# Routing search of the later experts in six passes of 3, 3, 3, 3, 2, 2 bits instead of eight of 2, with a place left out after a pass

## The chip, the cores and the metric

The kernel runs on one core of a Trainium2 chip. Its engines work side by side, each on its own queue in order: TensorE (PE in the rows, its weight loads PEld), VectorE (DVE), ScalarE (ACT), GpSimd (POOL), and SyncE (SP), which issues most transfers. The metric is device time in microseconds (us). The median of three runs before the change is 1104.6 us (1103.45 to 1105.63).

## The reference, cut to what matters

Three stages: windowed attention, a capacity-limited mixture of eight experts, a dense two-layer network. The change is in the routing of the mixture.

```python
logits = x @ w_gate                      # 3072 tokens, 8 experts
order = np.argsort(-logits.flatten())
for idx in order:                        # greedy: best pair first
    tok, e = idx // E, idx % E
    if assigned[tok] >= 0 or counts[e] >= cap:   # cap = 384
        continue
    assigned[tok] = e
    counts[e] += 1
...
for e in range(E):                       # own two layers, no overlap
    h = np.maximum(x[assigned == e] @ w1[e], 0.0)
    out[assigned == e] = h @ w2[e]
# then: h = x @ w_in; g = max(h, 0) + alpha * min(h, 0); g @ w_out
```

## The kernel before

Attention comes first and leaves the rows x in DRAM and the logits on the chip. Then `Experts.run` takes the experts one after the other, each with its 384 tokens in tiles of 3 x 128.

The greedy loop is replaced by phases, one for each expert (0 to 7). A phase finds the value of the 384th best pair of the expert that fills up next, marks that expert's tokens, turns them into a list, and closes the expert and the tokens in the logits. The value is a 32-bit key. `Router.phase` finds its upper 16 bits by one search and its lower 16 by a second; the last phase has no search, and phase 0 has one of its own (`first_search`), which the change leaves alone. So phases 1 to 6 make 12 searches.

A search (`Router.search`) makes eight passes, each of two bits. A pass compares all keys of a partition with three thresholds (`compare`, line 770: 8 experts x 3 thresholds x 24 tokens, 576 elements into `r_cmp`), adds them up along the tokens (`reduce`, line 778, into `r_red`), and adds up over the partitions by one small matmul on TensorE (`totals`, line 786, into `r_ps`). Then VectorE reads the totals (line 553, `r_mx`), counts the thresholds that are reached (line 556) and makes the next thresholds `r_thr` (line 564) and base (line 571) out of steps prepared beside the totals (`r_pre`, line 543). The last pass of a second search has four thresholds on float keys. A second search begins with `narrow` and `fill`, seven more small VectorE instructions.

The search is a generator, and its pieces are put between the matmuls. A yield follows the reduction and another follows the totals. An expert has 24 steps: 8 of its own first and second layer ("first-layer steps", matmuls on lines 923 and 950), and 16 of the dense network ("second-layer steps", lines 963 and 988). Step n issues the up-projection of step n+1 (12 matmuls) and then the down-projection of step n. A place for `next(gen)` stands at the start of a step, ahead of the up-projection, and one in the down-projection, ahead of its last third (`between`); two steps of an expert have none. That makes 44 places for an expert. All engines run in order, so TensorE stands still at the totals until the reduction is done, and VectorE takes up the evictions of a step's up-projection (lines 970 and 971 into `m_t`, or line 927 into `m_hh`) only behind the pieces issued before them. From `m_t` ScalarE makes the upper part of `m_g` (line 972) and GpSimd the lower part (line 973); the down-projection of the next step reads both. GpSimd also splits the experts' weights (line 891) and, for expert 0, the output weights (line 909). Late in an expert's second-layer steps the rows of the next expert are transposed (line 857) and evicted (lines 872 and 873).

The list of a phase takes six yields behind its searches: among them 24 small matmuls (line 704) on marks from VectorE (lines 686 to 697).

Of the kernel before, what the change touches and what calls it, by code (L numbers as in the profile page):

```python
# [9 lines left out]
FT = mybir.dt.float32  # L10
FR = mybir.dt.float32r
BF = mybir.dt.bfloat16
I32 = mybir.dt.int32
U32 = mybir.dt.uint32
U16 = mybir.dt.uint16
AF = mybir.ActivationFunctionType
OP = mybir.AluOpType
# [344 lines left out]
class Router:  # L362

    DIGITS = 3
    PASSES = 8
    BLOCK = 32
    CHUNK = 8
    CLOSED = 1.0e38
# [3 lines left out]
    def __init__(self, ctx, tc, logits, cap, n_experts, ident):  # L372
        nc = tc.nc
        self.nc, self.tc, self.L, self.cap, self.E = nc, tc, logits, cap, n_experts
        self.TT = logits.shape[1]
        E, TT, D = n_experts, self.TT, self.DIGITS
        assert cap == 3 * 128 and 2 * TT <= 128
        self.consts = consts = ctx.enter_context(tc.tile_pool(name="r_consts", bufs=1))
        self.m = consts.tile([128, TT], FT, name="r_m")
        self.flip = consts.tile([128, TT], I32, name="r_flip")  # L380
        self.key = consts.tile([128, TT], I32, name="r_key")
        halves = self.key.bitcast(U16).rearrange("p (t h) -> p t h", h=2)
        self.lo, self.hi = halves[:, :, 0], halves[:, :, 1]
        self.eq = consts.tile([128, E, TT], BF, name="r_eq")
        self.mk = consts.tile([128, E, TT], U16, name="r_mk")
        passes = self.HIGH + self.LOW
        self.cmp = consts.tile([128, max(E * (D + 1), max(d for d, _ in passes)) * TT], BF, name="r_cmp")
        both, at = consts.tile([128, sum(d for d, _ in passes)], U16, name="r_grid"), 0
        self.grids = []
        for d, _ in passes:  # L390
            self.grids.append(both[:, at:at + d])
            at += d
# [71 lines left out]
    def setup(self):  # L464
        nc, consts, E, TT, D = self.nc, self.consts, self.E, self.TT, self.DIGITS
        B = self.BLOCK
        NB = self.cap // B

        def iota(shape, dtype, name, pattern, base=0, slope=0):
            t = consts.tile(shape, dtype, name=name)  # L470
            nc.gpsimd.iota(t, pattern=pattern, base=base, channel_multiplier=slope,
                           allow_small_or_imprecise_dtypes=True)
            return t

        self.ones = consts.tile([128, 128], BF, name="r_ones")
        nc.vector.memset(self.ones, 1.0)
        self.before = consts.tile([128, 128], BF, name="r_before")
        nc.vector.memset(self.before, 1.0)
        nc.gpsimd.affine_select(self.before, self.before, pattern=[[1, 128]], compare_op=OP.is_gt, fill=0.0,
                                base=0, channel_multiplier=-1)  # L480
        self.slots = iota([128, B, TT], U16, "r_slots", [[1, B], [0, TT]])
        self.blocks = iota([128, NB, TT], U16, "r_blocks", [[1, NB], [0, TT]])
        yield
        self.tp = consts.tile([128, 2, TT], BF, name="r_tp")
        nc.gpsimd.iota(self.tp[:, 0], pattern=[[128, TT]], base=0, channel_multiplier=0,
                       allow_small_or_imprecise_dtypes=True)
        nc.gpsimd.iota(self.tp[:, 1], pattern=[[0, TT]], base=0, channel_multiplier=1,
                       allow_small_or_imprecise_dtypes=True)
        order = iota([128, E], FT, "r_order", [[-1, E]], base=E)
        self.flag = consts.tile([128, E, 5], FT, name="r_flag")  # L490
        nc.vector.tensor_scalar(self.flag[:, :, 4], order, 0.5 / E, None, op0=OP.mult)
        digits = iota([128, D, TT], FT, "r_digits", [[1, D], [0, TT]], base=1)
        self.last = iota([128, D + 1], FT, "r_last", [[1, D + 1]], base=1)
        yield
        for (d, size), g in zip(self.HIGH + self.LOW, self.grids):
            nc.gpsimd.iota(g, pattern=[[size, d]], base=size, channel_multiplier=0,
                           allow_small_or_imprecise_dtypes=True)
        yield
        ng = 128 // B
        rows = 2 * NB  # L500
        self.mask = consts.tile([rows, ng], BF, name="r_mask")
        t = iota([rows, ng], I32, "r_rows", [[-1, ng]], base=ng, slope=1)
        nc.vector.tensor_scalar(t, t, ng - 1, None, op0=OP.bitwise_and)
        nc.vector.tensor_scalar(self.mask, t, 0.0, None, op0=OP.is_equal)
        half = consts.tile([rows, 2, NB // ng], BF, name="r_half")
        t = iota([rows, 2, NB // ng], I32, "r_cols", [[-NB, 2], [-ng, NB // ng]], base=rows, slope=1)
        nc.vector.tensor_scalar(t, t, ng.bit_length() - 1, None, op0=OP.logical_shift_right)
        nc.vector.tensor_scalar(half, t, float(rows // ng), None, op0=OP.is_equal)
        self.unit = consts.tile([rows, NB // ng], BF, name="r_unit")
        nc.vector.tensor_tensor(self.unit, half[:, 0], half[:, 1], op=OP.add)  # L510
        yield
        self.steps = []
        for i in range(self.PASSES):
            step = consts.tile([128, D, TT], U16, name=f"r_step{i}")
            nc.vector.tensor_scalar(step, digits, self.size(i), None, op0=OP.mult)
            self.steps.append(step)
            if i % 3 == 2:
                yield
        yield
        self.ahead = consts.tile([128, 2 * TT], FT, name="r_ahead")  # L520
        nc.vector.memset(self.ahead, 0.0)
        self.units = consts.tile([128, 2 * TT], FT, name="r_units")
        nc.vector.memset(self.units, 1.0)

    def size(self, i):
        return float(4 ** (self.PASSES - 1 - i))

    def search(self, mk, result):
        nc, TT, D, w = self.nc, self.TT, self.DIGITS, self.work
        last = "top" in result  # L530
        thr, base, n = self.steps[0], None, self.PASSES
        for i in range(n):
            self.compare(result["full"] if last and i == n - 1 else mk, thr, 0, TT, TT)
            k = thr.shape[1]
            red = self.reduce(k)
            if last and i == n - 2:
                pre = w.tile([128, D + 1], FT, name="r_pre4")
                nc.vector.tensor_scalar(pre, self.last, base, None, op0=OP.add)
            elif i == 0:
                pre = self.steps[1]  # L540
            elif i < n - 1:
                pre = w.tile([128, D, TT], U16, name="r_pre")
                nc.vector.tensor_scalar(pre, self.steps[i + 1], base, None, op0=OP.add)
            if i == 0 and last:
                self.fill(result)
            yield
            cnt = self.totals(red, k)
            yield
            if last and i == n - 1:
                result["counts"], result["base"] = cnt, base  # L550
                return
            mx = w.tile([128, D], FT, name="r_mx")
            nc.vector.tensor_reduce(mx, cnt.rearrange("p e d -> p d e"), axis=AX.X, op=OP.max)
            ge = w.tile([128, D], FT, name="r_ge")
            dig = w.tile([128, 1], FT, name="r_dig")
            nc.vector.tensor_scalar(ge, mx, self.cap - 0.5, 0.0, op0=OP.is_ge, op1=OP.add, accum_out=dig)
            if i == n - 1:
# [2 lines left out]
                result["top"] = top  # L560
                return
            four = last and i == n - 2
            thr = w.tile([128, D + 1], FT, name="r_thr4") if four else w.tile([128, D, TT], U16, name="r_thr")
            nc.vector.scalar_tensor_tensor(thr, dig.to_broadcast([128, D + 1]) if four else  # L564
                                           dig[:, :, None].to_broadcast([128, D, TT]), self.size(i), pre,
                                           op0=OP.mult, op1=OP.add)
            nxt = w.tile([128, 1], FT, name="r_base")
            if base is None:
# [3 lines left out]
            base = nxt  # L572
# [200 lines left out]
    def reduce(self, d):  # L773
        nc, E = self.nc, self.E
        cmp = self.cmp[:, :E * d * self.TT].rearrange("p (e d t) -> p e d t", e=E, d=d)
        red = self.work.tile([128, E * 4], BF, name="r_red")[:, :E * d].rearrange("p (e d) -> p e d", d=d)
        with nc.allow_low_precision("counts up to 48 are exact in bfloat16"):
            nc.vector.tensor_reduce(red, cmp, axis=AX.X, op=OP.add)  # L778
        return red
# [19 lines left out]
class Experts:  # L799
# [206 lines left out]
    def run(self, router, n_experts):  # L1006
        nf1, nf2 = self.F1 // 128, self.F2 // 128
        routes = []
# [27 lines left out]
        def prepare(e, i):  # L1036
# [6 lines left out]
            else:  # L1043
                self.split_w2(e, 1)

        self.up1(0, 0)
        next(gen)
        self.split_w1(0, 2)
# [2 lines left out]
        for n, (e, s, f) in enumerate(steps):  # L1051
# [2 lines left out]
                self.load_w2(e, f + 3)  # L1054
            full = s == 1 and f == nf1 - 1 or s == 2 and f == 0
            if not full:
                next(gen, None)
            if s == 2 and chosen == e and len(routes) > e + 1 and "expert" in routes[e + 1]:
                chosen = e + 1
                self.choose(e + 1, routes[e + 1])  # L1060
# [21 lines left out]
                    self.split_w1(nx[0], nx[2] + 2)  # L1082
            for i in now:
                prepare(e + 1, i)
            (self.down1 if s == 1 else self.down2)(e, f, lambda: full or next(gen, None))
            if last:
                self.up2(e, 0)
            if s == 1 and f + 2 < nf1:
# [92 lines left out]
```

## Time and profile before

| | |
|---|---|
| median of three runs | 1104.6 us |
| the profiled execution | 1105.07 us |
| its span, first to last instruction | 1103.4 us |
| TensorE busy in the span | 1059.9 us (96%) |
| VectorE busy in the span | 761.8 us (69%) |
| GpSimd busy in the span | 516.1 us (47%) |

The rows are of one profiled execution. Times in rows count from the first instruction of the span. Busy time of TensorE holds its pipeline, and it is not the same as full use. Behind a duration stands, in brackets, idle time of the engine ahead of the instruction and what ended it. PEclk is the granted share of TensorE's clock, 1.00 being 2.4 GHz. A row of a stretch gives its bounds and length, then the busy us and the count of instructions of PE, PEld, DVE, ACT and POOL, then PEclk, the share of the transfer engines and GB/s. A row of a group ends with busy us, mean ns of one, and idle time ahead of it.

### The profile page before, as it was taken

Reading aid. Unit: us, or ns where it says so; the run is one execution under the profiler, and the core shown is the slowest. Engines: PE = TensorE matmul, PEld = TensorE weight load, DVE = VectorE, ACT = ScalarE, POOL = GpSimd, SP = SyncE. Lnnn points to the kernel's source line nnn. Section 1 sums busy time; section 2 is a strip of 40 time slices with the busy share of each in tenths; the row PEclk is TensorE's granted clock in tenths of the full one; section 3 lists DMA queues with packets and bytes.
Section 4 is the critical chain, followed back from the end, with each engine's and each line's share of the span. In section 5 each row is a group of like instructions: output and inputs, shape, how many; then the busy total and the mean of one; then the engine's idle time right before and its main releaser. Section 6 shows DMA issues by size and latency. Waiting matters only on the chain.

```text
span 1103.4 us, 19396 instructions
## 1 busy us (share of the span) xinstructions
PE 1059.9 (96%) x6658; PEld 939.1 (85%) x6659; DVE 761.8 (69%) x2228; ACT 401.4 (36%) x1001; POOL 516.1 (47%) x620
## 2 busy tenths in 40 slices
PE   8999999689999999999999999999999999999997
PEld 6877777559888988898889888988898999999995
DVE  7999999669879877887988798688752322231321
ACT  7999988223213321331133113312331232123211
POOL 4777776036457623542354326333533364246222
PEclk9999999769999999999999999999999999999998
DMA  9889985142244426334425333533354335334131
GB/s 221 221 234 229 230 239 134 30 120 66 110 172 143 163 77 200 105 134 142 155 96 182 125 115 115 162 131 125 99 162 143 134 98 194 130 115 162 64 127 67
DMA packets 151218, 156.54 MB, mean 142 GB/s; under 512 B 83536, under 2 KB 116304, under 8 KB 151120
## 3 DMA queue, kind: packets, MB, share of 16 engines
q1 hardware_dynamic: 147280, 142.72, 42.9%
q0 software_dynamic: 3840, 12.59, 3.4%
q8 instruction: 53, 0.87, 0.3%
q14 instruction: 45, 0.37, 0.1%
HBM read 134.31 MB, written 20.97 MB: 141 GB/s over the span
## 4 chain that ended last, share of the span: by engine, by line
PE 72%; DVE 14%; ACT 3%; issue 2%; DMA 1%; POOL 1%; SPq 0%; DVEq 0%; ACTq 0%; POOLq 0%
PE m_h L963 24%; PE m_acc L988 24%; PE m_acc L950 9%; PE m_h L923 9%; DVE a_sx L217 2%; DVE r_thr L564 2%; ACT a_p L220 2%; DVE r_red L778 1%; DVE r_cmp L770 1%; PE r_ps L704 1%; PE a_pt L231 1%; PE a_xp L247 1%; PE m_h L857 1%; PE a_s L211 1%; DVE f_t L78 1%
## 5 line engine op out<-in xcount | busy, mean ns | idle before, releaser
L973 POOL TENSOR_TENSOR m_g<-m_t,m_g 128x384 fp32r<-128x384 f32 (+1 forms) x144 | 139.8, 971 | 372.5 <-ACT m_g L972 370.5
L988 PE MATMUL m_acc<-m_so,m_g 128*128 128x512 f32 x1152 | 299.1, 400 | 0.3 <-POOL m_spacer L996 0.3
L963 PE MATMUL m_h<-m_y,wi 128*128 128x384 f32 x1536 | 294.1, 341 | 0.0
L963 PEld LDWEIGHTS m_h<-m_y,wi 128*128 128x128 f32 x1536 | 273.2, 189 | 7.6
L988 PEld LDWEIGHTS m_acc<-m_so,m_g 128*128 128x128 f32 x1152 | 209.5, 189 | 35.3 <-POOL m_g L973 0.8
L972 ACT ACTIVATE m_g<-m_t 128x384 fp32r<-128x384 f32 (+1 forms) x144 | 70.5, 490 | 435.6 <-DVE m_t L971 252.6
L891 POOL TENSOR_TENSOR m_s<-m_r,m_s 128x512 fp32r<-128x512 f32 x128 | 166.7, 1306 | 103.7 <-ACT m_s L890 103.5
L970 DVE TENSOR_SCALAR m_t<-m_h,m_al 128x384 f32<-128x384 f32 (+1 forms) x144 | 82.1, 570 | 149.1 <-PE m_h L963 138.9
L950 PE MATMUL m_acc<-m_hh,m_s 128*128 128x384 f32 x768 | 150.3, 340 | 1.3 <-DVE m_hh L927 1.3
L923 PE MATMUL m_h<-m_xt,m_s 128*128 128x384 f32 x768 | 145.9, 338 | 0.0
L923 PEld LDWEIGHTS m_h<-m_xt,m_s 128*128 128x128 f32 x768 | 136.3, 190 | 1.9 <-DVE m_xt L873 0.4
L950 PEld LDWEIGHTS m_acc<-m_hh,m_s 128*128 128x128 f32 x768 | 132.4, 188 | 2.9 <-DVE m_hh L927 1.6
L890 ACT ACTIVATE m_s<-m_r 128x512 fp32r<-128x512 f32 x128 | 79.7, 626 | 99.2 <-PE m_acc L950 33.9
L220 ACT ACTIVATE a_p<-a_sx,a_mn 128x232 f32<-128x232 f32 (+1 forms) x192 | 88.7, 471 | 17.0 <-DVE a_mn L217 16.7
L927 DVE SCALAR_TENSOR_TENSOR m_hh<-m_h,m_hh 128x384 fp32r<-128x384 f32 x64 | 35.3, 552 | 76.3 <-ACT m_hh L926 76.3
L971 DVE SCALAR_TENSOR_TENSOR m_t<-m_h,m_t 128x384 f32<-128x384 f32 (+1 forms) x144 | 73.9, 513 | 4.9
L778 DVE TENSOR_REDUCE r_red<-r_cmp 128x24 bf16<-128x576 bf16 (+1 forms) x97 | 73.8, 761 | 3.4
L217 DVE CUSTOM_DVE_ANT_0 a_sx<-a_s,a_bias 128x232 f32<-128x232 f32 (+1 forms) x192 | 61.4, 375 | 7.2 <-PE a_s L211 6.3
L926 ACT ACTIVATE m_hh<-m_h 128x384 fp32r<-128x384 f32 x64 | 31.5, 492 | 95.4 <-PE m_h L923 82.3
L770 DVE TENSOR_TENSOR r_cmp<-r_mk,r_thr 128x576 bf16<-128x576 uint16 x78 | 62.1, 797 | 0.0
L211 PE MATMUL a_s<-a_kz,a_qz 64*128 64x232 f32 (+1 forms) x384 | 48.9, 375 | 9.2 <-POOL a_kz L189 8.6
L231 PE MATMUL a_pt<-ident,a_p 128*128 128x128 f32 x352 | 50.1, 282 | 0.2
(183 smaller groups left out, 1256.2 us busy)
## 6 DMA issues: line engine op xcount, KB each, us to landing
m_so<-wo_pairs SPq DMA_DIRECT2D x112, 512.0 KB, 3.4
m_r<-in_moe_w_dram SPq DMA_DIRECT2D x128, 256.0 KB, 3.0
f_raw<-in_moe_w_in_dram SPq DMA_DIRECT2D x16, 512.0 KB, 4.1
f_raw<-in_moe_w_out_dram SPq DMA_DIRECT2D x16, 512.0 KB, 4.2
wo_pairs<-m_so SPq DMA_DIRECT2D x16, 512.0 KB, 2.7
a_k<-in_k_dram SPq DMA_DIRECT2D x24, 256.0 KB, 4.8
a_q<-in_q_dram SPq DMA_DIRECT2D x24, 256.0 KB, 5.2
a_v<-in_v_dram SPq DMA_DIRECT2D x24, 256.0 KB, 4.7
```

The lines of the kernel that those rows point to most:

```text
L217: nc.vector.tensor_tensor_reduce(out=sx[:, s, :n], in0=ps[s][:, a, :n], in1=bs[:, h], scale=-scale, scalar=BIG, op0=OP.add, op1=OP.min, ac ...
L220: nc.scalar.activation(pr[:, s, 2 * C - n:], sx[:, s, :n], AF.Exp, bias=T["mn", g][:, h:h + 1], scale=-1.0, accum_out=T["sum", g][:, h:h + 1])
L778: nc.vector.tensor_reduce(red, cmp, axis=AX.X, op=OP.add)
L890: self.nc.scalar.activation(s[:, 0], r, AF.Copy)
L891: self.nc.gpsimd.tensor_tensor(s[:, 1], r, s[:, 0], op=OP.subtract)
L923: nc.tensor.matmul(ps[:, :n], s1[:, a, d], x[:, b, d], start=(d == 0 and i == 0), stop=(d == self.ND - 1 and i == 2))
L950: nc.tensor.matmul(ps[:, :n], s2[:, b, d * 128:(d + 1) * 128], h[:, a], start=(f == 0 and a + b == 0), stop=(last and a == 1))
L963: nc.tensor.matmul(ps[:, :n], self.wi[:, a, d, f * 128:(f + 1) * 128], y[:, b, d], start=(d == 0 and i == 0), stop=(d == self.ND - 1 and i ...
L970: nc.vector.tensor_scalar(t[:, cs], ps[:, cs], 0.0, self.al[:, f:f + 1], op0=OP.min, op1=OP.mult)
L971: nc.vector.scalar_tensor_tensor(t[:, cs], ps[:, cs], 0.0, t[:, cs], op0=OP.max, op1=OP.add)
L973: nc.gpsimd.tensor_tensor(g[:, 1, cs], t[:, cs], g[:, 0, cs], op=OP.subtract)
L988: nc.tensor.matmul(ps, g[:, a, t * 128:(t + 1) * 128], s[:, b], start=(f == 0 and a + b == 0), stop=(last and a == 1))
```

## The change

The 16 bits are searched in six passes of 3, 3, 3, 3, 2 and 2 bits, with 7, 7, 7, 7, 3 and 3 thresholds (the last pass of a second search keeps its four). A pass of seven thresholds compares and adds up 1344 elements. The six rows of steps are written by GpSimd directly. From phase 2 on (`len(routes) > 2`), the place that follows a pass's reduction is left empty; phase 1 uses every place as before.

```diff
-    PASSES = 8
+    DOWN = ((7, 8192), (7, 1024), (7, 128), (7, 16), (3, 4), (3, 1))
...
-        digits = iota([128, D, TT], FT, "r_digits", [[1, D], [0, TT]], base=1)
...
-        for i in range(self.PASSES):
-            step = consts.tile([128, D, TT], U16, name=f"r_step{i}")
-            nc.vector.tensor_scalar(step, digits, self.size(i), None, op0=OP.mult)
-            self.steps.append(step)
+        for i, (d, size) in enumerate(self.DOWN):
+            self.steps.append(iota([128, d, TT], U16, f"r_step{i}", [[size, d], [0, TT]], base=size))
...
-        thr, base, n = self.steps[0], None, self.PASSES
+        thr, base, n = self.steps[0], None, len(self.DOWN)
...
-                pre = w.tile([128, D, TT], U16, name="r_pre")
+                pre = w.tile([128, 8, TT], U16, name="r_pre")[:, :self.DOWN[i + 1][0]]
...
-            yield
+            yield "rest"
             cnt = self.totals(red, k)
             yield
...
+            else:
+                d = self.DOWN[i + 1][0]
+                thr = w.tile([128, 8, TT], U16, name="r_thr")[:, :d]
+                times = dig[:, :, None].to_broadcast([128, d, TT])
+            nc.vector.scalar_tensor_tensor(thr, times, self.size(i), pre,
                                            op0=OP.mult, op1=OP.add)
...
+        self.rested = True
+
+        def slot():
+            if not self.rested and len(routes) > 2:
+                self.rested = True
+            else:
+                self.rested = next(gen, None) != "rest"
+
...
             if not full:
-                next(gen, None)
+                slot()
...
-            (self.down1 if s == 1 else self.down2)(e, f, lambda: full or next(gen, None))
+            (self.down1 if s == 1 else self.down2)(e, f, lambda: full or slot())
```

## Rows read from the trace of the kernel before

**Rows 1.** The page, first part: busy us and share of each engine.

```profile
PE 1059.9 (96%) x6658; PEld 939.1 (85%) x6659; DVE 761.8 (69%) x2228; ACT 401.4 (36%) x1001; POOL 516.1 (47%) x620
```

**Rows 2.** Stretches: second-layer step without and with a pass; first-layer step with a wait.

```profile
944.52:948.71 4.19, 4.19 (x23) 3.80 (x22) 1.18 (x2) 0.24 (x2) 1.02 (x1) 1.00 0.41 125
...
404.63:408.95 4.32, 4.32 (x23) 3.75 (x22) 3.91 (x12) 0.53 (x1) 1.01 (x1) 1.00 0.37 127
...
683.32:688.44 5.12, 4.45 (x26) 4.14 (x26) 5.05 (x7) 1.64 (x3) 3.67 (x3) 1.00 0.40 139
```

**Rows 3.** Waits of TensorE, 240.4 to 820 us: who, for whom, total, times, longest.

```profile
PE r_ps L786 <- DVE r_red L778: 3.5, 6, 0.7
```

**Rows 4.** Timeline of a second-layer step: start, length, engine, line, operation, tiles.

```profile
403.81 0.19 PE L786 MATMUL r_ps<-r_red,r_ones 128*128 128x24 bf16 x1
...
404.02 0.53 ACT L972 ACTIVATE m_g<-m_t 128x384 fp32r<-128x384 f32 x1 [3.83 <-PE r_ps L786]
...
404.04 0.18 DVE L553 TENSOR_REDUCE r_mx<-r_ps 128x3 f32<-128x24 f32 x1
...
404.62 1.02 POOL L973 TENSOR_TENSOR m_g<-m_t,m_g 128x384 fp32r<-128x384 f32 x1 [3.31 <-ACT m_g L972]
...
404.73 1.23 DVE L770 TENSOR_TENSOR r_cmp<-r_mk,r_thr 128x576 bf16<-128x576 uint16 x1
...
405.99 0.75 DVE L778 TENSOR_REDUCE r_red<-r_cmp 128x24 bf16<-128x576 bf16 x1
...
406.75 1.55 PE L988 MATMUL m_acc<-m_so,m_g 128*128 128x512 f32 x6
...
407.02 0.62 DVE L970 TENSOR_SCALAR m_t<-m_h,m_al 128x384 f32<-128x384 f32 x1
```

**Rows 5.** VectorE groups by line and form: count, busy us, mean ns.

```profile
L778 DVE TENSOR_REDUCE r_red<-r_cmp 128x24 bf16<-128x576 bf16 x90 | 67.8, 753 | 3.1
...
L778 DVE TENSOR_REDUCE r_red<-r_cmp 128x32 bf16<-128x768 bf16 x6 | 5.7, 953 | 0.2
...
L694 DVE TENSOR_TENSOR r_sl<-r_slots,r_in 128x256 bf16<-128x256 uint16 x3 | 0.8, 283 | 0.0
```

**Rows 6.** Lines 770 and 564, ns min/median/max; one comparison of 768 in the timeline.

```profile
L564 DVE SCALAR_TENSOR_TENSOR r_thr<-r_dig,r_pre x72: 162/234/2494, 246.2 to 778.7; 128x72 uint16<-128x72 f32 x66, 128x4 f32<-128x4 f32 x6
...
L770 DVE TENSOR_TENSOR r_cmp<-r_mk,r_thr x78: 445/459/2033, 236.0 to 774.3; 128x576 bf16<-128x576 uint16 x78
...
323.31 0.54 DVE L694 TENSOR_TENSOR r_sl<-r_slots,r_in 128x768 bf16<-128x768 uint16 x1
```

**Rows 7.** Timeline of first-layer steps of expert 0, DVE, POOL and PE.

```profile
246.17 1.06 DVE L564 SCALAR_TENSOR_TENSOR r_thr<-r_dig,r_pre 128x72 uint16<-128x72 f32 x1
...
248.56 0.19 PE L786 MATMUL r_ps<-r_red,r_ones 128*128 128x24 bf16 x1
...
252.73 1.17 DVE L543 TENSOR_SCALAR r_pre<-r_step,r_base 128x72 uint16<-128x72 uint16 x1
...
254.43 1.29 POOL L891 TENSOR_TENSOR m_s<-m_r,m_s 128x512 fp32r<-128x512 f32 x1 [0.57 <-ACT m_s L890]
...
254.68 1.12 DVE L564 SCALAR_TENSOR_TENSOR r_thr<-r_dig,r_pre 128x72 uint16<-128x72 f32 x1
```

**Rows 8.** Timeline where a second search begins beside the transposes for expert 3.

```profile
562.69 0.55 DVE L873 TENSOR_TENSOR m_xt<-m_h,m_xt 128x384 fp32r<-128x384 f32 x1
...
563.15 0.61 DVE L970 TENSOR_SCALAR m_t<-m_h,m_al 128x384 f32<-128x384 f32 x1
...
564.45 0.52 ACT L972 ACTIVATE m_g<-m_t 128x384 fp32r<-128x384 f32 x1 [5.62 <-DVE r_mx L553]
...
565.02 1.65 PE L988 MATMUL m_acc<-m_so,m_g 128*128 128x512 f32 x6
```

**Rows 9.** Stretches: the two steps of expert 0 around the list of expert 1.

```profile
319.69:326.92 7.23, 6.32 (x46) 5.38 (x45) 5.76 (x13) 2.09 (x4) 3.13 (x3) 0.95 0.85 262
...
326.92:332.66 5.74, 5.74 (x24) 5.06 (x22) 1.80 (x6) 0.78 (x2) 1.56 (x3) 0.76 0.47 186
```

More of the change, by code (lines that the diff above doesn't have):

```diff
@@ L386, in __init__ @@
         passes = self.HIGH + self.LOW
-        self.cmp = consts.tile([128, max(E * (D + 1), max(d for d, _ in passes)) * TT], BF, name="r_cmp")
+        self.cmp = consts.tile([128, max(E * max(D + 1, max(d for d, _ in self.DOWN)), max(d for d, _ in passes)) * TT], BF, name="r_cmp")
         both, at = consts.tile([128, sum(d for d, _ in passes)], U16, name="r_grid"), 0
@@ L525, in size @@
     def size(self, i):
-        return float(4 ** (self.PASSES - 1 - i))
+        return float(self.DOWN[i][1])
     def search(self, mk, result):
@@ L551, in search @@
                 return
-            mx = w.tile([128, D], FT, name="r_mx")
+            mx = w.tile([128, 8], FT, name="r_mx")[:, :k]
             nc.vector.tensor_reduce(mx, cnt.rearrange("p e d -> p d e"), axis=AX.X, op=OP.max)
-            ge = w.tile([128, D], FT, name="r_ge")
+            ge = w.tile([128, 8], FT, name="r_ge")[:, :k]
             dig = w.tile([128, 1], FT, name="r_dig")
@@ L562, in search @@
             four = last and i == n - 2
-            thr = w.tile([128, D + 1], FT, name="r_thr4") if four else w.tile([128, D, TT], U16, name="r_thr")
-            nc.vector.scalar_tensor_tensor(thr, dig.to_broadcast([128, D + 1]) if four else
-                                           dig[:, :, None].to_broadcast([128, D, TT]), self.size(i), pre,
+            if four:
+                thr, times = w.tile([128, D + 1], FT, name="r_thr4"), dig.to_broadcast([128, D + 1])
+            else:
[3 more added lines that the diff above has]
+            nc.vector.scalar_tensor_tensor(thr, times, self.size(i), pre,
                                            op0=OP.mult, op1=OP.add)
@@ L775, in reduce @@
         cmp = self.cmp[:, :E * d * self.TT].rearrange("p (e d t) -> p e d t", e=E, d=d)
-        red = self.work.tile([128, E * 4], BF, name="r_red")[:, :E * d].rearrange("p (e d) -> p e d", d=d)
+        red = self.work.tile([128, E * 8], BF, name="r_red")[:, :E * d].rearrange("p (e d) -> p e d", d=d)
         with nc.allow_low_precision("counts up to 48 are exact in bfloat16"):
```

## The prediction

> **What bounds the kernel now.** The page comes first: TensorE is busy in 96% of the span, VectorE in 69% [rows 1]. So other engines cost time only where TensorE stands still for them or gets more to do. Next come the stretches of single steps. A second-layer step takes 4.19 us without a search and 4.32 with one pass in it, TensorE being busy throughout in both [rows 2]: a pass costs it the totals, 0.13 us. A first-layer step of 5.12 us holds 4.45 of TensorE's work [rows 2]: here it stood still. The waits say how often that is so for the routing: six times for a reduction ahead of the totals, 3.5 us together [rows 3]. The rest of VectorE's work for the routing is hidden now. The question is what stays hidden when it comes in larger pieces.
>
> **What a long pass costs VectorE.** A reduction of 576 elements takes 753 ns and one of 768 takes 953 [rows 5], so 1.04 ns an element: 1344 elements take 1.55 us, 0.80 more. The comparison alone takes 459 ns [rows 6]. Comparisons of 16-bit values took 283 ns for 256 elements [rows 5] and 0.54 us for 768 [rows 6], so 0.50 ns an element: 0.39 more. (At the reduction's rate it would be 0.80; I take the same kind of instruction.) Thresholds and steps have 96 elements more each: 0.10 more for each of the two at 1.04, or nothing; reading the totals 0.03. A long pass is thus 1.42 us longer (1.2 to 1.85). A short one lasts from 404.04 to 406.74 in the timeline [rows 4], 2.70 us to the end of its reduction; a long one 2.70 + 0.03 + 0.10 + 0.39 + 0.80 = 4.02.
>
> There are 12 searches. Two passes fewer in each save VectorE 24 x 2.9 = 70 us (2.70 and 0.23 for the next steps), and 48 long ones add 48 x 1.42 = 68. VectorE's work stays the same; it is cut into larger pieces, and the number of totals falls.
>
> **Totals.** 24 fewer at 0.13 [rows 2] are -3.1 us. 48 become 32 columns wider; six matmuls of 512 columns took 1.55 us [rows 4], 0.5 ns a column, so 48 x 0.016 = +0.8. Together **-2.3**.
>
> **Waits ahead of the totals.** All six [rows 3] lie in phases 2 to 6, where a place will be left out between reduction and totals; that is more time than the longest wait. **-3.5**, at worst 0.
>
> **Phase 1, which leaves no place out.** Its passes stay one to a step. Two of its eight long ones come ahead of step 0, five in the first-layer steps of expert 0, one in a second-layer step. In the first of the five the thresholds waited until 246.17 + 1.06 = 247.23; with 0.46 and 0.75 behind them the reduction ended at 248.5, and the totals ran at 248.56, right behind it [rows 4, 6, 7]. With seven thresholds: 247.33, then 0.85 and 1.55, so 249.8; TensorE stands still for 1.25 us. In the steps behind it VectorE now waits for GpSimd twice: preparing steps takes 1.17 us and the thresholds, of the same 72 elements, 1.12 [rows 7], against 0.23 alone [rows 6], so 1.8 us of waiting. The growth of 1.42 fits into that if the comparison still starts ahead of GpSimd's split of 1.29 us [rows 7]; if it falls behind it, the totals come 1.1 to 1.3 late. Worked forward from these rows, the two fall due within some 0.2 us of each other, so I take half of the four: 2 x 1.2. **+3.7**, between 1.3 and 5 x 1.3 = 6.5. For this choice the Trainium skill has a rule (SBUF — State Buffer, "Who interferes with whom"): an instruction of VectorE with two inputs in SBUF and one of GpSimd that reads SBUF exclude each other, and the one issued first holds the ports to its end. The trace agrees: the comparison took 1.23 us beside GpSimd's 1.02 [rows 4] and 0.46 elsewhere. By it a pass is late by all or by nothing, which gives 1.3 or 6.1, and nothing between except as a mean over passes. The two passes ahead of step 0 I cost at nothing, because the rows of expert 0 are still on their way from DRAM; with that cover gone they are 2 x 1.3.
>
> **Late evictions.** A pass issued at the first place of a step delays that step's m_t. It begins 0.59 us ahead of the step (404.04 against 404.63), and with 4.02 ends 3.4 into it; m_t began 2.4 into it (407.02) [rows 2, 4]. That is 1.1 late with the next steps. In the row the upper half of m_g is done at 404.55 and the down-projection reads it at 406.75 [rows 4]: 2.2 us of slack, so nothing is paid. Where a second search begins there is no slack left: m_t starts at 563.15 behind m_xt, the upper half ends at 564.97, and the down-projection starts at 565.02 [rows 8]. There 0.39 + 0.80 more are paid in full. From phase 2 on a phase takes 12 x 3 + 6 = 42 of 44 places (38 before), so no expert lacks its list. Phase 2 begins at place 27 of expert 0, and second searches 18 places later: place 1 and 43 of expert 1, 41 of expert 2, 39 of expert 3, 37 of expert 4. The last two lie beside transposes: 2 x 1.15. The other three I take at nothing (at most 1.2 each). The first pass of phase 2, beside gathers and the output weights' splits, loses its wait for the totals and gets a late m_t for it; between 0 and 1.2, I take 0.9. **+3.2** (0 to 7.2). Transposes add 0.55 us to VectorE's step [rows 8], where long passes fill the rest: **+0.5** (0 to 2).
>
> **Long passes at a second place.** With three places to a pass, each second one starts behind the step's m_t, 3.65 us into the step, and its reduction ends 3.65 + 4.02 - 4.19 = 3.48 into the next; the totals' place is at 4.33 - 0.82 = 3.51 [rows 2, 4]. That is a margin of 0.03. For 20 of 40 passes I take **+0.5** in all, between 0 and 20 x 0.35 = 7.
>
> **Clock.** At the list of expert 1 TensorE stood still for 0.91 us (7.23 with 6.32 busy), the granted clock fell, to 0.76 over the next step, and that step took 5.74 instead of 4.3 [rows 9]. The list now comes eight places earlier, so the same may or may not happen: half of the 1.4 it cost, rounded, **-0.6**.
>
> GpSimd's iotas and VectorE's eight dropped step instructions lie in attention, far from its bound; nothing.
>
> **Sum.** -2.3 - 3.5 + 3.7 + 3.2 + 0.5 + 0.5 - 0.6 = +1.5 on the profiled execution's 1105.07 is 1106.6. That execution lies 0.5 above the median, so **1106.1 us**.
>
> **Rivals.**
> *A, the waits swallow the growth* (faster). VectorE's 1.8 us of waiting for GpSimd in a first-layer step [rows 7] is time it can use; only the first long pass is late, and slack covers the evictions: -2.3 - 3.5 + 1.3 - 0.6 = -5.1, 1099.5. Against it: the comparison itself is what waits for GpSimd in the second layer [rows 4].
> *B, long passes at a second place come late* (slower). It decides at 0.03 us: if a reduction ends later than I worked out, say behind a second GpSimd instruction, TensorE waits in 20 passes, 0.35 each: +7, less the 0.5 above: 1112.6. For it speaks the longest comparison, 2.03 us [rows 6].
> *C, the waits in phase 1 lower the clock* (slower). A standstill of 0.91 us with small matmuls behind it did [rows 9]; four waits of 1.2 at about 1.3 each: +5, 1111. Against it: the wait of 5.12 - 4.45 = 0.67 us in a first-layer step left it at 1.00 [rows 2]. The Trainium skill's rule (TensorE: Matmul & The Clock Gate, "What's actually happening") is that the low clock is the default and activity lifts it, so idle time would count twice; the trace agrees at the one place [rows 9] and not at the other [rows 2].
> *D, the change does not do what it says.* A search of six passes at three places is 18 places, more than 16, so routing gets no shorter. If neither waits nor lateness change, the totals alone remain: 1102.3.
>
> **Chances and range.** Forecast 0.40, A 0.20, B 0.22, C 0.10, D 0.08. A measurement of this kernel can tell about 0.2%, 2.2 us, from no change. The forecast with its own range, 1102.4 to 1106.8, is no change: 0.40. A and D are faster: 0.28. B and C are slower: 0.32. Both signs hold most of the chance, so the range reaches into A and B: 1099.5 to 1112.
>
> **What would show it.** Right: 73 totals instead of 97; reductions of about 1.55 us and comparisons of 0.85 when alone; waits of TensorE for the reduction of 1.1 to 1.3 us between 246 and 275 us, three or four of them, and nearly none from phase 2 on; VectorE's busy time within a few us of 761.8; second-layer steps of 4.2 and 4.3. Wrong: no such wait in phase 1 (A), many short ones at the totals of later phases (B), or PEclk below 0.9 in expert 0's first layer (C).

## Result and the profile after

The changed kernel takes **1112.66 us** (median of 5 runs, 1110.13 to 1113.96) beside 1104.6 for the kernel before: ratio 1.0069, with a 95% interval of 1.0051 to 1.0087. It is slower by more than the 0.2% that can be told apart, against a forecast of no change, and its time lies just above the range. The profiled execution took 1112.66 us, its span is 1110.9.

The page of the kernel after, first part, answers to [rows 1]:

```profile
PE 1055.9 (95%) x6635; PEld 937.4 (84%) x6635; DVE 749.4 (67%) x2028; ACT 400.6 (36%) x1001; POOL 523.4 (47%) x625
```

TensorE has 4.0 us less to do and the span is 7.5 us longer. So the loss is standstill, not work. The waits of TensorE, 240 to 920 us (total, times, longest), answer to [rows 3]:

```profile
PE r_ps L787 <- DVE r_red L779: 12.6, 22, 1.5
PE r_ps L705 <- DVE r_val L698: 0.8, 1, 0.8
PE m_acc L989 <- ACT m_g L973: 0.8, 2, 0.6
```

The kind of wait that was to vanish has grown from 3.5 us in 6 times to 12.6 in 22. Where it lies is told by one row for each expert, from its first up-projection to the next expert's (length, then busy time of PE, PEld, DVE, ACT, POOL, then granted clock, DMA share, GB/s), experts 0 to 5 of the kernel after:

```profile
239.74:356.27 116.53, 110.00 (x576) 98.35 (x575) 94.64 (x213) 36.17 (x72) 67.25 (x55) 0.96 0.33 115
356.27:462.61 106.34, 105.70 (x581) 95.78 (x580) 80.36 (x188) 26.36 (x53) 47.84 (x45) 1.00 0.45 148
462.61:571.58 108.97, 106.08 (x582) 95.70 (x580) 82.66 (x185) 26.01 (x51) 45.03 (x43) 1.00 0.40 132
571.58:680.87 109.29, 106.70 (x581) 95.83 (x581) 81.72 (x189) 27.18 (x53) 45.05 (x43) 1.00 0.39 128
680.87:789.84 108.97, 106.43 (x582) 95.91 (x580) 84.64 (x185) 26.12 (x51) 45.73 (x44) 1.00 0.40 131
789.84:897.86 108.02, 106.94 (x601) 97.67 (x600) 61.23 (x149) 27.23 (x53) 44.18 (x43) 1.00 0.41 134
```

The kernel before had 111.7, 107.8, 107.4, 107.4, 108.4 and 106.8 here. Expert 0 lost 4.8 us, experts 1 to 5 together 3.8 (541.6 against 537.8). Expert 0's part holds for this execution: in the run skip_scatter below, whose code for expert 0 is the same, it takes 113.4 us, 1.7 more than before. In expert 2, for one, TensorE is idle for 2.9 us of 109.0.

Single steps show three kinds of place. Same view and kernel, three steps of phase 1 (expert 0, first layer), then the first pass of phase 2, two steps where a second search begins, and a first-layer step of expert 2:

```profile
250.53:255.78 5.25, 4.46 (x26) 4.14 (x26) 5.15 (x11) 1.65 (x3) 2.55 (x2) 1.00 0.31 98
264.37:270.01 5.64, 4.45 (x27) 4.14 (x26) 5.40 (x10) 1.65 (x3) 2.91 (x3) 1.00 0.03 10
270.01:275.45 5.44, 4.46 (x27) 4.14 (x27) 5.34 (x12) 1.12 (x2) 1.47 (x1) 1.00 0.00 0
318.18:323.77 5.59, 4.37 (x24) 3.72 (x22) 5.42 (x9) 0.25 (x1) 4.83 (x5) 1.00 0.33 110
566.12:571.58 5.46, 4.37 (x24) 3.63 (x22) 5.30 (x7) 0.41 (x1) 2.23 (x2) 1.00 0.18 55
571.58:576.93 5.35, 4.82 (x23) 3.76 (x23) 2.79 (x7) 2.05 (x4) 2.59 (x4) 1.00 0.01 2
471.24:477.15 5.91, 4.45 (x26) 4.13 (x26) 5.88 (x5) 1.65 (x3) 4.25 (x4) 1.00 0.49 152
```

In all but the sixth, VectorE is busy for nearly the whole step, its waits beside GpSimd included, while TensorE's work is 4.4 to 4.5 us: VectorE sets the length. The sixth pays for the fifth: its gate product comes late.

VectorE's instructions by form (count, busy us, mean ns, idle ahead), after, answer to [rows 5, 6]:

```profile
L779 DVE TENSOR_REDUCE r_red<-r_cmp 128x56 bf16<-128x1344 bf16 x48 | 74.5, 1553 | 1.7
L771 DVE TENSOR_TENSOR r_cmp<-r_mk,r_thr 128x1344 bf16<-128x1344 uint16 x36 | 50.8, 1411 | 0.0
...
L771 DVE TENSOR_TENSOR r_cmp<-r_mk,r_step 128x1344 bf16<-128x1344 uint16 x12 | 10.3, 858 | 0.4
```

The long reduction takes 1.553 us (worked out beforehand: 1.55) and the comparison alone 0.86 (0.85). But the 36 comparisons with computed thresholds take 1.41 on average: most of them run beside GpSimd. The worst of them, the timeline of the step at 471.24 (start, length, engine, line, operation, tiles):

```profile
470.61 0.97 POOL L998 DMA_INDIRECT out_dram<-m_x,r_idx  x1 [0.22 <-ACT m_s L891]
...
471.17 3.69 DVE L771 TENSOR_TENSOR r_cmp<-r_mk,r_thr 128x1344 bf16<-128x1344 uint16 x1
...
471.61 2.53 POOL L892 TENSOR_TENSOR m_s<-m_r,m_s 128x512 fp32r<-128x512 f32 x2
...
474.90 1.55 DVE L779 TENSOR_REDUCE r_red<-r_cmp 128x56 bf16<-128x1344 bf16 x1
...
476.51 0.20 PE L787 MATMUL r_ps<-r_red,r_ones 128*128 128x56 bf16 x1 [1.46 <-DVE r_red L779]
```

The comparison is issued while GpSimd scatters the previous expert's output (L998). Behind the scatter stand two weight splits without a gap, and the comparison ends 0.7 us behind the second, 2.8 us later than alone. TensorE waits 1.46 us.

Where a second search begins, the timeline of 566 to 572:

```profile
566.14 0.99 DVE L579 TENSOR_SCALAR r_over<-r_key,r_top 128x24 f32<-128x24 uint16 x1
567.05 1.34 DVE L581 SCALAR_TENSOR_TENSOR r_part<-r_key,r_top 128x24 f32<-128x24 uint16 x1
...
569.03 0.86 DVE L771 TENSOR_TENSOR r_cmp<-r_mk,r_step 128x1344 bf16<-128x1344 uint16 x1
569.93 1.55 DVE L779 TENSOR_REDUCE r_red<-r_cmp 128x56 bf16<-128x1344 bf16 x1
...
571.54 0.20 PE L787 MATMUL r_ps<-r_red,r_ones 128*128 128x56 bf16 x1 [1.09 <-DVE r_red L779]
...
572.22 0.61 DVE L971 TENSOR_SCALAR m_t<-m_h,m_al 128x384 f32<-128x384 f32 x1
```

The new keys (r_over to r_mk) are prepared at the same place as the first comparison, 2.9 us ahead of it. Two of these instructions wait beside GpSimd: 0.99 and 1.34 us, against at most 0.24 each in short_first_skip below. At the starts of 670 and 774 us the same two take 0.99 and 1.33. Even with one place left out the reduction ends at 571.48, behind TensorE's arrival at the totals. So this step pays by the totals and the next one by the late m_t.

### The profile page after: what moved, and what is told of

Its sections match the earlier page's. It is cut to its first block, busy times and chain, and to the rows that moved or that the text cites. A ratio compares the mean times of both kernels' runs of the same rounds, so it can differ in the third digit from the quotient of the medians.

```text
span 1110.9 us, 19155 instructions
## 1 busy us (share of the span) xinstructions
PE 1055.9 (95%) x6635; PEld 937.4 (84%) x6635; DVE 749.4 (67%) x2028; ACT 400.6 (36%) x1001; POOL 523.4 (47%) x625
## 4 chain that ended last, share of the span: by engine, by line
PE 64%; DVE 20%; issue 5%; ACT 3%; POOL 2%; DMA 1%; SPq 0%; DVEq 0%; POOLq 0%; ACTq 0%
PE m_h L964 19%; PE m_acc L989 17%; PE m_acc L951 10%; PE m_h L924 10%; DVE r_cmp L771 4%; DVE r_red L779 3%; DVE a_sx L217 1%; PE a_pt L231 1%; PE a_s L211 1%; PE a_xp L247 1%; PE r_ps L705 1%; DVE r_thr L566 1%; DVE m_t L971 1%; DVE m_t L972 1%; ACT a_p L220 1%
## 5 line engine op out<-in xcount | busy, mean ns | idle before, releaser
L964 PEld LDWEIGHTS m_h<-m_y,wi 128*128 128x128 f32 x1536 | 270.0, 189 | 10.4 <-issue 2.2
L892 POOL TENSOR_TENSOR m_s<-m_r,m_s 128x512 fp32r<-128x512 f32 x128 | 171.0, 1339 | 98.5 <-ACT m_s L891 98.3
L951 PE MATMUL m_acc<-m_hh,m_s 128*128 128x384 f32 x768 | 146.2, 337 | 0.5 <-DVE m_hh L928 0.5
L779 DVE TENSOR_REDUCE r_red<-r_cmp 128x56 bf16<-128x1344 bf16 (+2 forms) x73 | 94.2, 1290 | 2.5
L771 DVE TENSOR_TENSOR r_cmp<-r_mk,r_thr 128x1344 bf16<-128x1344 uint16 (+1 forms) x54 | 59.0, 1093 | 0.0
L247 PE MATMUL a_xp<-a_pts,a_v 128*64 128x128 f32 x704 | 49.4, 280 | 0.6 <-DVE a_xt L253 0.5
```

Of the source, the lines that this page charges most:

```text
L771: nc.vector.tensor_tensor(self.flags(d, t0, n, chunk), mk[:, :, None, t0:t1].to_broadcast([128, E, d, n]), thr[:, None].to_broadcast([128, ...
L892: self.nc.gpsimd.tensor_tensor(s[:, 1], r, s[:, 0], op=OP.subtract)
L951: nc.tensor.matmul(ps[:, :n], s2[:, b, d * 128:(d + 1) * 128], h[:, a], start=(f == 0 and a + b == 0), stop=(last and a == 1))
L964: nc.tensor.matmul(ps[:, :n], self.wi[:, a, d, f * 128:(f + 1) * 128], y[:, b, d], start=(d == 0 and i == 0), stop=(d == self.ND - 1 and i ...
```

## Experiments

Three theories, by what they blame. **Theory 1**: phase 1, whose passes leave no place out. **Theory 2**: the starts of second searches (and of phase 2), where preparation and a long pass come from one place. **Theory 3**, formed after the first four runs: long passes that meet the scatter and the splits behind it. The rival to all three is that the passes as such cost time, through clock or evictions. Times are set against the kernel before on the same chip (1105.84, 1105.09 and 1105.52 us in the three groups of runs).

**p1_short**: phase 1 keeps eight passes of 2 bits.

```diff
+    FIRST, LATER = SHORT, LONG        # SHORT: eight times (3, 4**k)
...
-                yield from self.search(self.mk, found)
+                plan = self.FIRST if k == 1 else self.LATER
+                yield from self.search(self.mk, found, plan)
```

> Phase 1 searches with eight passes of three thresholds as before; phases 2 to 6 as in the changed kernel. Theory 1 (phase 1 without free places costs what the prediction's term for it says, and a bit more, 4.8 us in the steps of expert 0): these steps fall back to about 112 us, four totals come back (+0.5), so about 1108.3 us. Rival (the loss is all in phases 2 to 6, and expert 0's steps are longer for the clock alone): 1111.5 to 1113.

Measured 1116.95 us, ratio 1.0103 [1.0081, 1.0125]. Expert 0 came back to 111.4 us, as theory 1 says. But phase 2 now begins eight places later, and experts 1 to 5 took 548.2 us instead of 541.6, so the total missed the 1108.3 that was expected. Most of the loss lies in expert 1 and is taken up under shift8.

**p1_long_only**: the counterpart, six passes in phase 1, eight of 2 bits afterwards, no place left out.

```diff
+    FIRST, LATER = LONG, SHORT
...
-            if not self.rested and len(routes) > 2:
+            if not self.rested and False:
```

> The six-pass search in phase 1 alone; phases 2 to 6 with eight passes and no free place, as before. Theory 1: expert 0's steps take about 116.5 us as in the changed kernel, the rest as before, so 1109 us, and no wait of TensorE for a reduction over 0.8 us behind expert 0. Rival (loss in phases 2 to 6 alone): 1104 to 1105.

Measured 1109.19 us, ratio 1.0034 [1.0023, 1.0045]. The total is as expected. The steps of phase 1 take 5.91, 5.64 and 5.44 us again, so they are phase 1's own; the step of 5.25 takes 4.32 here. Experts 1 to 5 need 538.3 us, as before the change: the 3.8 us come with the long passes of phases 2 to 6. Expert 0 took 112.3 us in the profile, not the 116.5 that was expected. The profiled execution is the fastest of eight (1105.94 us), and its granted clock did not fall at the list of expert 1, where the two steps took 6.74 and 4.51 us (7.33 and 5.54 in the changed kernel's profile).

**split_starts**: from phase 2 on, one more place between preparing the keys and the first comparison of each search.

```diff
             self.candidates(0, TT)
+            if k > 1:
+                yield
...
                 self.narrow(found)
+                if k > 1:
+                    yield
                 yield from self.search(self.mk, found)
```

> As the changed kernel, but from phase 2 on the first comparison of each search gets a place of its own, one behind the instructions that prepare its keys; a phase then takes 44 places of 44. Theory 2 (in phases 2 to 6 the loss sits where a second search begins, 7 us over the five, because preparation, long comparison and long reduction come as one piece): the steps at these places come back to 4.2 to 4.6 us, and the time falls by 5 to 7 us, to 1106 to 1108. Rival (it is spread over the long passes that begin at a second place, as rival B had it): no more than 1 us less, 1111.5 to 1113.

Measured 1128.01 us, ratio 1.0209 [1.0183, 1.0235]. This is a miss in the total: the starts did get back to 4.2 to 4.3 us, but the longer phase moved the second search of each of experts 1 to 5 to the scatter, and the third first-layer step of each took 7.1 us. In experts 1, 2 and 4 the next step then took 5.6 to 5.8 us at a granted clock of 0.71 to 0.74 (4.25 at 1.00 in expert 3), and at the list in expert 5 TensorE waited twice more, 1.9 and 2.2 us. At the scatter, in the timeline:

```profile
472.59 3.02 DVE L556 TENSOR_TENSOR r_top<-r_dig,r_base 128x1 f32<-128x1 f32 x1
...
473.02 2.55 POOL L896 TENSOR_TENSOR m_s<-m_r,m_s 128x512 fp32r<-128x512 f32 x2
```

An instruction of 128x1 elements takes 3.02 us: it holds VectorE until the second split has ended. This run gave theory 3: it is not the comparison's size that counts there, any such instruction can be caught, and a long pass has no room left behind it.

**no_rest**: no place is left out at all.

```diff
-            if not self.rested and len(routes) > 2:
+            if not self.rested and False:
```

> As the changed kernel, but no place is ever left free. Theory (VectorE's work for a long pass with the evictions of a step, 5.5 us, is more than a step of 4.3, so each of the 40 long passes of phases 2 to 6 costs about 1 us): 1140 to 1160 us. Rival (the waits of VectorE for GpSimd swallow it, and a place left free only shifts the pass): within 3 us of 1112.7.

Measured 1144.74 us in one run; TensorE waits 34.7 us in 35 times for the reduction. The extra places are needed: without them the time is 32 us longer.

**short_first**: the 2-bit pass comes first instead of fifth, so each search begins with a short comparison and reduction.

```diff
-    DOWN = ((7, 8192), (7, 1024), (7, 128), (7, 16), (3, 4), (3, 1))
+    DOWN = ((3, 16384), (7, 2048), (7, 256), (7, 32), (7, 4), (3, 1))
```

> As the changed kernel, with the bits in the order 2, 3, 3, 3, 3, 2: as many passes, places and thresholds, but the pass with which a search begins has three thresholds instead of seven. Theory 2 (where a second search begins, seven small instructions, a long comparison and a long reduction in one place make the totals of the next place late and then the evictions): the steps at 566, 571, 670, 676 and 774 us, together 5.9 us too long, come back to within 1 us, so does the first step of phase 2 (1.3), and the time falls by 5 to 8 us. Rival (it matters only which pass meets GpSimd's scatter of the expert before, in the first three steps of an expert): within 2 us of the changed kernel.

Measured 1106.3 us, ratio 1.0011 [1.0001, 1.002]. The same number of passes and places, only reordered, comes out some 6 us below the change. The start at 566 us takes 4.26 instead of 5.46, the first step of phase 2 4.38 instead of 5.59. Experts 1 to 5 need 536.4 us; first-layer steps of 5.95 (at 469.80) and 5.22 stay. Of the five steps that were to come back to within 1 us, 2.1 us stay: the step behind each start is still late (5.35 at 568.73, 4.83 at 671.70), and the start beside transposes takes 5.25.

**skip_scatter**: the changed kernel, but from expert 1 on no routing is issued at two places in a row, the second of first-layer step 0 and the first of step 1, while GpSimd scatters.

```diff
-            if not full:
+            if not full and not (e and s == 1 and f == 1):
                 slot()
...
-            (self.down1 if s == 1 else self.down2)(e, f, lambda: full or slot())
+            (self.down1 if s == 1 else self.down2)(e, f, lambda: full or (e and s == 1 and f == 0) or slot())
```

> As the changed kernel, but from expert 1 on the second place of an expert's step 0 and the first of its step 1 stay empty, where GpSimd issues the scatters of the expert before and then three splits in a row; 42 places remain and a phase takes 42. Theory 3 (VectorE's instructions with two inputs wait there up to 3.7 us, and a long pass makes TensorE wait for it): the steps 1 and 2 of experts 1 to 5, together 4.5 us too long, come back, and the time falls by 2 to 5 us unless the second search, which now begins at step 2, loses as much. Rival (theory 2 alone): no gain from these steps, within 1.5 us.

Measured 1107.93 us, ratio 1.0027 [1.0017, 1.0038]. TensorE's waits for the reduction fell to 6.0 us, but a new one appeared, five times: the second search now begins right ahead of the scatter, and its rank instruction is caught in place of the comparison. Timeline of expert 2:

```profile
468.89 3.24 DVE L594 SCALAR_TENSOR_TENSOR r_rank<-r_key,r_top,r_rest 128x24 f32<-128x24 uint16 x1
...
469.54 2.54 POOL L892 TENSOR_TENSOR m_s<-m_r,m_s 128x512 fp32r<-128x512 f32 x2
```

The up-projection's m_hh comes late by that (waits of 6.4 us in all). Experts 1 to 5 stay at 542.2 in the profile. Of these, 3.1 us are the clock's: in experts 2 and 3 the next step took 5.81 and 5.82 us at a granted clock of 0.71, and 4.27 at 1.00 in expert 4. This execution (1110.63 us) is the slowest of eight.

**shift8**: phase 2 begins eight places later, everything else as in the change.

```diff
+            if k == 2:
+                for _ in range(8):
+                    yield
             self.candidates(0, TT)
```

> As the changed kernel, but phase 2 begins eight places later, where it began in the run with a short phase 1. Theory 3 (what counts is which step a long pass falls on): the steps of experts 1 to 5 come to about what they took in that run, 548 us against 540 in the changed kernel. Rival (the short phase 1 was slower for another reason): 538 to 542.

Measured 1114.75 us in one run; experts 1 to 5 need 542.7. Which expert pays changes (expert 4 now 110.5, with a step of 7.12 us at the scatter; expert 3 108.6 instead of 109.3), the sum hardly does: it lies near the rival's 538 to 542, not at 548. So the later start by itself explains only 1 of the 6.6 us that p1_short lost there. Of the other 5.5, 4.4 lie in three steps of expert 1 of p1_short (5.15, 6.17 and 5.83 us; here 4.32, 4.20 and 4.25). There GpSimd scatters later, and a comparison of only three thresholds is issued into the scatter, with four splits behind it:

```profile
364.75 4.75 DVE L775 TENSOR_TENSOR r_cmp<-r_mk,r_thr 128x576 bf16<-128x576 uint16 x1
...
365.41 5.22 POOL L896 TENSOR_TENSOR m_s<-m_r,m_s 128x512 fp32r<-128x512 f32 x4
```

It takes 4.75 us; here the same comparison comes behind the splits, at 369.03, and takes 0.45. TensorE waits 1.81 us for it, and the step behind (5.83) ran at a granted clock of 0.71. So theory 3 explains most of what p1_short lost, and 1.1 us are not settled.

**short_first_skip**: both edits.

> Both: the order 2, 3, 3, 3, 3, 2 and the two empty places. If theories 2 and 3 both hold, experts 1 to 5 take 533 to 536 us (the kernel before: 538), and the time is 1101 to 1105; if either fails, 1106 or more.

Measured **1099.02 us** (1098.12 to 1099.84), ratio **0.9948** [0.9932, 0.9965]: faster than both kernels and than expected. Experts 0 and 2 in the view by expert, columns as above:

```profile
240.65:354.91 114.26, 107.90 (x575) 95.98 (x575) 96.80 (x213) 36.10 (x72) 67.66 (x54) 0.98 0.33 117
...
460.69:566.19 105.50, 105.50 (x580) 95.74 (x579) 76.66 (x181) 26.49 (x52) 46.81 (x44) 1.00 0.41 135
```

TensorE's busy time is the whole length of expert 2, and so it is in experts 1 and 3 to 5: nothing waits there any more. Experts 1 to 5 take 529.3 us, 12.3 less than in the change. Each edit by itself had left the other's cost standing or moved it. The ranks, which were caught at 468.89 in skip_scatter, now run ahead of the last scatter, behind a short pass:

```profile
467.78 0.24 DVE L594 SCALAR_TENSOR_TENSOR r_rank<-r_key,r_top,r_rest 128x24 f32<-128x24 uint16 x1
...
468.24 0.97 POOL L998 DMA_INDIRECT out_dram<-m_x,r_idx  x1 [0.22 <-issue]
```

The empty places also moved the starts: with 42 places for a phase of 42, a search begins at the same step of every expert, and its preparation no longer waits beside GpSimd (skip_scatter has this too). No run separates this from the scatter. Expert 0 is still 2.6 us above the kernel before, though here the clock did not fall at the list.

**before_skip**: the same two empty places in the kernel before.

```diff
-            if not full:
+            if not full and not (e and s == 1 and f == 1):
                 next(gen, None)
...
-            (self.down1 if s == 1 else self.down2)(e, f, lambda: full or next(gen, None))
+            (self.down1 if s == 1 else self.down2)(e, f, lambda: full or (e and s == 1 and f == 0) or next(gen, None))
```

> The kernel before with the same two places left empty from expert 1 on. In the kernel before, four steps beside the scatter took 5.17, 4.58, 4.48 and 5.12 us, together 2.4 us more than 4.25 each. Theory (the empty places only take the scatter's collisions away, the wider passes bring the rest): these steps fall to 4.2 to 4.3, experts 1 to 5 together to 534 to 536 us, ratio 0.997 to 0.999. Rival (the empty places alone make the gain of the kernel with both edits, and fewer passes give nothing): ratio 0.994 to 0.996. Second rival (a phase of eight passes needs the places, its later steps then come late against the list): no gain, ratio 1.000 or more.

Measured 1102.18 us, ratio 0.9969 [0.996, 0.9978], as the first theory had it. The scatter's steps take 4.29 us, experts 1 to 5 534.5. So the empty places alone, with passes of 2 bits, gain 3.4 us of the 5.7 that short_first_skip gains. With them the wider passes add 5.2 us in experts 1 to 5 and lose part of it again in expert 0; without them (short_first) the wider passes gain nothing.

**p1_short_rest**: short_first_skip with phase 1 back at eight passes of 2 bits.

> The kernel that beat both (bits 2, 3, 3, 3, 3, 2 and two empty places from expert 1 on), with phase 1 back at eight passes of 2 bits; phases 2 to 6 then begin 8 places later. Theory (the empty places follow the scatter, not the phase, so the shift costs nothing now): expert 0 back from 114.3 to 111 to 112 us, experts 1 to 5 still 528 to 531, ratio 0.992 to 0.994. Rival (the shift puts the second search or a 3-bit first comparison beside another burst of GpSimd, as it did without the empty places): experts 1 to 5 at 533 to 545, ratio 0.997 or more.

Measured 1117.35 us, ratio 1.0114 [1.0099, 1.013]. Expert 0 took 111.7 us as hoped, the others 549.9, more than the rival gave. The scatter is caught once more, one step further on: its last indirect DMA runs to 472.4 us, four splits follow, and in the timeline of VectorE

```profile
474.62 3.04 DVE L569 SCALAR_TENSOR_TENSOR r_thr<-r_dig,r_pre 128x168 uint16<-128x168 f32 x1
```

holds up a long pass (that step takes 5.67 us); it ends 0.2 us behind the fourth split. The empty places are tied to a step number, and here GpSimd was still busy behind them. The list and the gather come later as well: TensorE waits five times each for m_y (3.0 us in all), for gathered rows (2.3) and for m_g (1.8), which short_first_skip hardly knows. So the 20.6 us in experts 1 to 5 have several parts: 7.0 in the step that is caught, 4.8 in the step that waits for m_y, 9.2 in two late second-layer steps at the gather, less what other steps save.

## Why the prediction failed

**Sizes of the instructions: right.** Reduction 1.553 us, comparison alone 0.858, 73 totals, totals of 56 columns 0.20 us against 0.19 [rows 4]. VectorE's busy time fell by 12.4 us, not by 2. I had priced the steps and thresholds of a dropped pass by their time alone, 0.23 us each. Beside GpSimd they take longer: 66 and 72 of them took 30.3 and 34.0 us before, 42 and 48 of them 15.4 and 22.3 after.

**Waits ahead of the totals, -3.5: the step that failed.** I took a place left out to be "more time than the longest wait". That compared the wait of a short pass with the spare time of a long one, as if the pass could be late by no more than before. Three of the six waits (1.4 us) lay in other steps of experts 2 to 4, and they are gone, as forecast: their steps took 4.78, 4.94 and 5.17 us (at 558.05, 589.07 and 703.21) and take 4.40, 4.21 and 4.29. A fourth, at the first pass of phase 2, grew from 0.69 to 1.22 us and is taken up with the starts below. The last two (1.4 us) lay beside the scatter, and there the opposite of the forecast came. In the kernel before the scatter's steps of experts 1 to 4 took 5.17, 4.58, 4.48 and 5.12 us, [rows 2] showing the last; after, the longest there take 5.00, 5.91, 4.74 and 4.75, and 5.37 in expert 5. That is 1.1 us more in experts 1 to 4 and 1.1 (over 4.25) in expert 5, so +2.2. With the 1.4 us that went the term comes to +0.8 instead of -3.5.

In experts 1 and 2 one VectorE instruction is caught there (ranks of 3.23 us, the comparison of 3.69); in experts 3 to 5 one or two wait for one split each (1.07 to 1.58 us). A long pass has 4.0 us of its own. The instructions of 3.02, 3.24, 3.04 and 4.75 us in four runs show that the size does not decide; short_first_skip and before_skip, with no such instruction at that place, show the loss gone. The kernel before had the same, once in each of experts 1 to 4 (3.16, 2.41, 2.49 and 2.43 us), with only a short pass behind. Its timeline:

```profile
360.89 3.16 DVE L571 SCALAR_TENSOR_TENSOR r_base<-r_dig,r_base 128x1 f32<-128x1 f32 x1
...
575.94 2.49 DVE L564 SCALAR_TENSOR_TENSOR r_thr<-r_dig,r_pre 128x72 uint16<-128x72 f32 x1
```

So I had the row: the thresholds of 2.49 in [rows 6]. (The comparison of 2.03 there stood beside expert 0's gather, at 236.00.) I took them for scattered cases instead of asking what stood beside them and what would be put there next.

The Trainium skill (SBUF — State Buffer, "Who interferes with whom") says that issue order, not the shape of the operation, decides who blocks. The 3.02 us for 128x1 elements agree with it.

**Late evictions, +3.2: mis-sized, +6.1.** Starts at 566.12 and 571.58 (5.46, 5.35), 670.54 and 675.73 (5.19, 5.14) exceed the 4.32 of a step with a pass [rows 2] by 3.9 us together; the one beside transposes at 774.24 (6.43) exceeds such a step's 4.66 by 1.8; the first pass of phase 2 takes 5.59, 0.4 more than before (5.19). I had priced two starts by a late m_t, and the start at 566 us, "at nothing", cost most, 2.2. What was overlooked is that a start is late at both ends: the totals of the long pass wait too (1.09, 0.70, 0.70 and, in phase 2's first, 1.22 us), since its comparison stands behind 2.9 us of preparation, of which 1.9 us are waits beside GpSimd at the three starts. short_first, which shortens only that pass, brought steps of 5.46 and 5.59 to 4.26 and 4.38.

**Phase 1, +3.7: right in mechanism, its size hangs on the clock.** In this execution the first eight steps of expert 0 grew by 3.8 us. Four long passes wait for the totals (0.42, 0.80, 1.19, 0.98), and their steps are 1.3, 0.9, 1.3 and 1.1 longer. The first of these steps holds more than its wait: the granted clock was 0.83 in it, and TensorE's own work took 5.47 us (4.57 before, at 1.00). In skip_scatter, with the same code in phase 1, the clock was 1.00 there and the whole wait fell on this step, 1.36 us. The first row is the changed kernel, the second skip_scatter:

```profile
244.64:250.53 5.89, 5.47 (x27) 5.16 (x27) 5.12 (x10) 2.02 (x4) 3.09 (x3) 0.83 0.65 178
```

```profile
244.45:250.36 5.91, 4.54 (x27) 4.23 (x27) 5.12 (x11) 2.03 (x4) 3.82 (x4) 1.00 0.64 177
```

There three of the five passes wait (1.36, 1.19, 0.96) and two do not, as the prediction had it, and the eight steps grew by 2.2 us. The pass ahead of step 0, taken at nothing, waited 2.6 us in the changed kernel, yet step 0 began at 239.74, no later than before (240.41); it is 0.7 longer. Against all this 1.5 us came back that I had not seen: in the kernel before a second search began in the last first-layer step and made m_hh 1.25 late (that step took 7.93 us, now 6.41).

**Second place, +0.5; transposes, +0.5; clock, -0.6.** Eight passes at a second place waited 0.16 to 0.18 us, 1.3 in all; rival B's twenty of 0.35 did not come. Four steps beside transposes take 18.3 us against 18.8 before in expert 1: no loss. TensorE stood still at the list of expert 1 again (0.82 us), and the step after it, from 312.64, ran at a granted clock of 0.79; the two steps take 7.33 and 5.54 us against 7.23 and 5.74 [rows 9], so the clock term is nothing here. In skip_scatter, the same code in expert 0, the clock did not fall at the list and the two take 6.85 and 4.47: "may or may not happen" was right.

**The rivals.** The slower side came, but not as B (the second place). C came in small part: 0.9 us in the step at 244.64, and the clock was back at 1.00 from 250 us on. The terms found in experts 1 to 5, 2.2 for the scatter, 5.7 for the starts and 1.3 for the second place, less 1.4 for the three waits that went and 1.9 for the totals as worked out, make 5.9, and 3.8 was measured: the other steps saved some 2 us more that are not broken down.

## What to carry to other kernels

When work that hides beside another engine is cut into larger pieces, ask for each place in the order what else runs there, not what it costs on average: a burst on a neighbouring engine can hold one instruction for most of its length, and a larger piece has no slack left behind it. Look at the longest instance of an instruction and at what stands beside it; that place is worth an empty slot before any piece is made wider. An empty place between late work and its reader helped here, but skip_scatter and p1_short_rest show that the work which it displaces can land on the next burst: test both edits together, as each alone may show little. And set steps against steps, not totals alone: with the same code, expert 0 took 113.4 and 116.5 us in two executions, most of it by the clock that was granted.

## Unexpected in the hardware

An instruction of VectorE with two inputs that was issued while GpSimd's indirect scatter ran (about 1 us) waited through the two weight splits behind it as well: 3.02 us for 128x1 elements, 3.24 for 128x24, 3.69 for 128x1344. The first two end within 0.1 us of the second split's end, the third 0.7 behind it, which leaves it about its own 0.86. With four splits behind the scatter one of 128x576 took 4.75 us (p1_short); issued into four splits in a row, one of 128x168 took 3.04 and ended 0.2 behind the last. In the kernel before, the thresholds at 575.94 began 0.2 us behind the scatter's end and waited through both splits too, so the scatter itself need not be what holds them. It is not always so: in the changed kernel thresholds issued at 581.30, 0.4 us into the first of two splits, took 1.07 us and ended between the two. What decides between the two cases is open.
